# Attention, expert and dense layers in one kernel: one-hot rows by one scaled operation and a transfer, constants in six groups, similarities behind the products with v

## The chip, the cores and the metric

The kernel runs on one core of one Trainium2 chip. Its engines are TensorE (PE, matrix products and transposes), ScalarE (ACT), VectorE (DVE), GpSimd (POOL) and SyncE (SP, which here issues most of the transfers, or DMAs). The metric is the time of one execution on the device in microseconds (us), given as the median of several runs. All engines run their own queues of instructions in order; they wait for each other by semaphores.

## The reference

Three layers follow each other. All numbers are float32.

```python
# attention: 2 batches x 8 heads, 768 tokens, 64 wide, 16 clusters per head
q_assign = argmax(q_n @ c_n.T); k_assign = argmax(k_n @ c_n.T)     # rows normalised
scores = where(q_assign == k_assign, scale * q @ k.T, -1e9)
attn = exp(scores - max(scores)); attn = attn / (attn.sum() + 1e-9)
x = attn @ v                                                      # 1536 tokens x 512
# experts: each token goes to the best of 8
logits = x @ w_gate + modality_bias[modality_id]; e = argmax(logits)
x[t] = softmax(logits)[e] * (relu(x[t] @ w1[e]) @ w2[e])          # 512 -> 1024 -> 512
# dense: four experts, weighted
out = sum over e of p[:, e] * (relu(x @ w1b[e]) @ w2b[e])
```

## The kernel before, in words

Heads are worked on in pairs (p = 0 to 7, heads 2p and 2p+1). For each pair q and k are loaded, transposed on PE (`tr`, tile `pq`), copied by ACT to `xf` and split into a high and a low part in `hl` (ACT makes the high part, L308, DVE the low one). `stack` then copies them by SP's transfers into one stacked operand for each head, `st`: 128 partitions and four slots of 768 columns, so that one matmul over 128 rows and one over 80 give a tile of scores.

The mask sits in the 80-row matmul. `sims` multiplies q and k with the normalised centroids (`pm`), `simn`, `best` and `first` find the best cluster of each token with DVE and POOL, and write its one-hot to `oht`. `troh` transposes that (`po`, 112 rows: 16 for q and 16 for k of each head, at 0, 32, 64 and 96) and writes rows 64 to 79 of `st`: -BIG times q's one-hot in slot 0, and in slot 3 a 1 where the cluster isn't k's. A pair of tokens of unlike clusters so gets -BIG added to its score.

A head has six score tiles of 128 x 768 (`scores`, tile `s`, L406 and L407). For each, DVE takes the maximum (`nm`, L411), ACT the exponential (`e`, L417, with the row sums), PE transposes `e` (`t`, L429), ACT or DVE copy it to `at`, and after six tiles PE multiplies by v (`o`, L446). Score tiles have two buffers in the PSUM memory, so tile i+2 waits until the exponential has read tile i. Names in the traces and lists carry the head and the tile: `s4_0` is head 4, tile 0.

The order is written in a table of steps, `OFF`: six steps are a head, twelve a pair, and `put(step, prio, f)` files each function at a step counted from the start of its pair; within a step the priority decides. From the order in which the functions are then called a list scheduler fixes each engine's queue. `issue_after` adds an order between two instructions, `high_priority` moves instructions ahead. Beside the pairs stands the list `extra`: small constants, the routing of the first batch (transposing x, logits, choice of expert, positions, a scatter through DRAM by POOL), its reading back in sorted order (`reload`, `sorted_xT`). Then come the expert slots (`ph`: w1, `ht`: relu; `pa`, `pb`: w2, L780 to L796) and the dense layer. Its input is prepared during the last expert slot (`dense_x`: `turn` transposes, `sums` are subtractions on POOL at L1008, `ready` casts them on ACT at L1016), by the list `todo`, one entry per stage of that slot.

## Time and profile before

| | |
|---|---|
| median of three runs | 982.63 us (979.29, 982.63, 983.04) |
| profiled execution | 981.43 us, span 979.7 us |
| granted TensorE clock, mean | 0.991 of full speed |
| busy PE, DVE, ACT, POOL | 945.3, 603.4, 476.0, 382.3 us |
| share of the chain that ended last | PE 52%, every other engine 1% or less |
| largest groups on PE | dense layer's second product (L1105) 276.9 us; transposes of `e` 87.7; experts' first product 78.2; score tiles 74.2 and 68.4 |

The span runs from the first to the last instruction. Busy shares are averages over stages of different kind: up to about 300 us the attention, to 486 us mostly the experts, then the dense layer. Idle time of an engine counts only if the engine that sets the end waits for it.

### The profile page before, as it was taken

The page shows a single profiled execution, that of the slowest core. Times are in us where ns is not written, and L with a number is a line of the kernel's source. Part 1 is how long each engine was busy: PE and PEld are TensorE (multiplying, and loading weights), DVE is VectorE, ACT ScalarE, POOL GpSimd, SP SyncE. Part 2 cuts the span into 40 slices and gives each one's busy share as a digit, 9 for nine tenths or more (in the row PEclk, how much of TensorE's full clock was granted, in tenths as well). Part 3 has the DMA queues.
Part 4 walks back from the last instruction along what each step waited for, and adds up shares of the span by engine and source line. Part 5 has one row for each costly group of instructions (what it writes and reads, how often), then busy time and mean ns, then how long its engine had stood idle before and what let it go on. Part 6 is the DMA issues. An engine that isn't in the chain of part 4 may idle for free.

```text
span 979.7 us, 14022 instructions
## 1 busy us (share of the span) xinstructions
PE 945.3 (96%) x5199; PEld 788.5 (80%) x5199; DVE 603.4 (62%) x1050; ACT 476.0 (49%) x920; POOL 382.3 (39%) x404
## 2 busy tenths in 40 slices
PE   8899999989999999989999999999999999999997
PEld 6666766666667788877889989898998989898896
DVE  7876777667775355463666565656766565665654
ACT  7778777767773242354534333343533334343320
POOL 6524531534000400026594544545344544535302
PEclk9999999999999999999999999999999999999999
DMA  8553456076122870266212121222213212212201
GB/s 176 119 133 78 98 130 141 22 198 177 42 88 87 311 235 31 74 215 191 71 62 77 55 85 65 64 66 64 65 65 108 65 65 65 65 65 65 65 1 64
DMA packets 80244, 95.87 MB, mean 98 GB/s; under 512 B 29616, under 2 KB 59824, under 8 KB 80176
## 3 DMA queue, kind: packets, MB, share of 16 engines
q1 hardware_dynamic: 77248, 85.40, 31.0%
q0 software_dynamic: 2784, 9.54, 2.6%
q8 instruction: 41, 0.67, 0.3%
q14 instruction: 27, 0.22, 0.1%
q10 hardware_dynamic: 144, 0.03, 0.0%
HBM read 70.53 MB, written 6.34 MB: 78 GB/s over the span
## 4 chain that ended last, share of the span: by engine, by line
PE 52%; DVE 1%; POOL 1%; DMA 1%; issue 1%; SPq 1%; ACT 0%; POOLq 0%; DVEq 0%; ACTq 0%
PE po L1105 26%; PE px L1057 13%; PE pz L1057 7%; PE py L1057 3%; PE ph L780 1%; DMA rw<-in_moe_w_dram 1%; PE pa L796 1%; POOL out_dram L1142 0%; DVE hd L1064 0%; POOL t L1008 0%; DVE w L749 0%; PE pxT L999 0%; PE pb L796 0%; POOL xf L1008 0%; SPq L921 0%
## 5 line engine op out<-in xcount | busy, mean ns | idle before, releaser
L1105 PE MATMUL po<-w,hd 128*128 128x512 f32 x1152 | 276.9, 393 | 1.3 <-DVE y L1140 1.3
L1105 PEld LDWEIGHTS po<-w,hd 128*128 128x128 f32 x1152 | 215.5, 188 | 46.3 <-DVE y L1140 1.7
L1140 DVE SCALAR_TENSOR_TENSOR y<-po,meta,y 128x512 f32<-128x512 f32 x180 | 132.0, 746 | 56.7 <-PE po L1105 56.7
L1041 POOL TENSOR_TENSOR wa<-rw,wa 128x512 fp32r<-128x512 f32 (+1 forms) x62 | 68.8, 1129 | 173.2 <-PE po L1105 92.0
L411 DVE TENSOR_REDUCE nm<-s 128x1 f32<-128x768 f32 x96 | 91.0, 952 | 27.4 <-PE s L407 26.9
L1040 ACT CAST ws<-sw 128x1024 fp32r<-128x1024 f32 x31 | 32.6, 1050 | 146.4 <-PE po L1105 123.2
L749 DVE TENSOR_TENSOR w<-rw,w 128x1024 fp32r<-128x1024 f32 x63 | 78.4, 1247 | 37.4 <-ACT w L748 37.1
L748 ACT CAST w<-rw 128x1024 fp32r<-128x1024 f32 x63 | 65.8, 1050 | 65.6 <-PE pz L1057 35.1
L417 ACT ACTIVATE e<-s,nm 128x768 f32<-128x768 f32 x96 | 87.3, 909 | 14.8 <-DVE nm L411 13.1
L429 PE MATMUL t<-ident,e 128*128 128x128 f32 x576 | 87.7, 278 | 2.5 <-DVE at L435 1.5
L780 PE MATMUL ph<-x,w 128*128 128x384 f32 x384 | 78.2, 354 | 5.5 <-DVE ht L784 3.0
L406 PE MATMUL s<-st 128*128 128x384 f32 x192 | 74.2, 387 | 9.0 <-ACT e L417 8.4
L429 PEld LDWEIGHTS t<-ident,e 128*128 128x128 f32 x576 | 69.8, 142 | 12.5 <-ACT at L433 3.1
L780 PEld LDWEIGHTS ph<-x,w 128*128 128x128 f32 x384 | 70.5, 197 | 10.1 <-issue 4.5
L1041 POOL TENSOR_TENSOR ws<-sw,ws 128x1024 fp32r<-128x1024 f32 x31 | 74.6, 2407 | 9.9 <-ACT ws L1040 9.4
L1057 PE MATMUL px<-xd,wa 128*128 128x384 f32 x384 | 78.0, 338 | 0.0
L1057 PE MATMUL px<-xd,ws 128*128 128x384 f32 x384 | 77.8, 337 | 0.1
L1057 PE MATMUL pz<-xd,ws 128*128 128x384 f32 x384 | 77.5, 337 | 0.0
L407 PE MATMUL s<-st 80*128 80x384 f32 x192 | 68.4, 357 | 3.6 <-ACT st L396 3.6
L1057 PEld LDWEIGHTS px<-xd,wa 128*128 128x128 f32 x384 | 68.6, 188 | 3.1 <-issue 0.2
L1057 PEld LDWEIGHTS pz<-xd,ws 128*128 128x128 f32 x384 | 68.2, 188 | 2.9 <-ACT xf L1000 0.2
L446 PE MATMUL o<-at,vraw 128*64 128x384 f32 x384 | 70.1, 502 | 0.0
(262 smaller groups left out, 1456.5 us busy)
## 6 DMA issues: line engine op xcount, KB each, us to landing
rw<-in_moe_w_dram SPq DMA_DIRECT2D x94, 512.0 KB, 3.5
st<-hl SPq DMA_DIRECT2D x46, 384.0 KB, 6.9
lw<-in_moe_w_dram SPq DMA_DIRECT2D x16, 512.0 KB, 5.7
xs<-xs_sorted POOLq DMA_DIRECT2D x2, 1560.0 KB
qraw<-in_q_dram SPq DMA_DIRECT2D x16, 192.0 KB, 3.4
kraw<-in_k_dram SPq DMA_DIRECT2D x16, 192.0 KB, 4.0
vraw<-in_v_dram SPq DMA_DIRECT2D x8, 384.0 KB, 4.0
xs_sorted<-x,r_posi POOLq DMA_INDIRECT x12, 7.2
```

What stands on the lines that cost most here:

```text
L406: t.matmul(ps[:, j, 0:384], st[:, 1, qc], st[:, 2, kc], start=True, stop=False)
L407: m = t.matmul(ps[:, j, 0:384], st[0:80, 0, qc], st[0:80, 3, kc], start=False, stop=True)
L411: self.mark = v.tensor_reduce(out=nm, in_=ps[:, :, 0:384], axis=AX.XY, op=ALU.max, negate=True)
L417: a.activation(e, ps[:, :, 0:384], AF.Exp, bias=nm, scale=1.0, accum_out=state[n]["sums"][:, i:i + 1])
L429: self.turned = t.transpose(pt[:, r, :], e[:, j, r * 128:(r + 1) * 128], self.ident)
L446: t.matmul(po[64 * hf:64 * hf + 64], vr[:, r], at[hf][:, r, :], start=(r == 0), stop=(r == R - 1))
L749: self.v.tensor_tensor(out=lo, in0=raw, in1=hi.bitcast(F32), op=ALU.subtract)
L780: t.matmul(ph, w[:, wi, kc, fs], x[:, :, kc, xi, :], start=(m == 0), stop=(m == 11))
L1041: g.tensor_tensor(out=w[:, 1, r], in0=src, in1=w[:, 0, r].bitcast(F32), op=ALU.subtract)
L1057: t.matmul(ps, w[:, wi, 2 * ai + k], xd[bi // 2][:, bi % 2, xi, k], start=start and m == 0, stop=m == 5, skip_group_check=not start)
L1105: t.matmul(p, d["h"][:, 2 * f + j, hi, 128 * i:128 * i + 128], W[2][:, wi, f, :], start=m == 0, stop=m == 5)
L1140: v.scalar_tensor_tensor(out=y, in0=p, scalar=pr, in1=y, op0=ALU.mult, op1=ALU.add)
```

## The change

1. For pairs 1 to 7, `troh` writes the transposed one-hots of all four groups with one ACT operation for each half into a tile `oh` of 112 rows, with a scale per row (`ohs`: -BIG on the rows of q, 1 elsewhere). Four SP transfers of 16 x 768 numbers (48 KB) take them to rows 64 to 79 of the two stacked operands. The copies of `hl` for the second head (`stack(p, 1)`) now come between the two pairs of transfers.
2. The steps: transposes of q and k at -14 and -13 rather than -13 and -12, the first head's stack at -8 rather than -4, the similarities at -12 and behind the last product with v (`self.grouped`), `troh` at -5; reading back, sorted x and the leftovers 3 or 4 steps later, and `sorted_xT` at every second step; the logits in two functions, routing at steps 0, 1, 2, 4, 6, 8 and 10 instead of every second.
3. `best` of pair 6 multiplies on DVE rather than on POOL.
4. The constants that were made at step 2 in one go are made in six groups at steps 3, 6, 9, 17, 20 and 23.
5. `todo` transposes one piece of the dense input per stage rather than two, and starts sums and casts three stages later.

```diff
-OFF = dict(load=-23, loadv=-9, loadv0=-3, norms=-17, tr0=-13, tr1=-12, st0=-4, sims=-11, simn=-9, best=-8,
-           first=-6, st1=-4, troh=-4, sc=-2, ex=-1, tt=0, av=6, fin=11, avn=2, nd=6, tpq=1, tpn=0, tpo=0, tot=0,
+OFF = dict(load=-23, loadv=-9, loadv0=-3, norms=-17, tr0=-14, tr1=-13, st0=-8, sims=-12, simn=-9, best=-8,
+           first=-6, st1=-5, troh=-5, ptroh=7, sc=-2, ex=-1, tt=0, av=6, fin=11, avn=2, nd=6, tpq=1, tpn=0, tpo=0, tot=0,
            pprep=7, pstack=5, pav=5, pfin=7, psc=0, pex=1, ptt=2, pno=8, t00=46, t01=50, t02=53, rs=53, rd=2,
-           rl=66, rld=75, sx=72, lf=83, lo=93, t10=92, s0w=90, s0=95, s0n=4, t13=98)
+           rl=70, rld=78, sx=75, lf=86, lo=93, t10=92, s0w=90, s0=95, s0n=4, t13=98)
...
+        self.ohs = self.const([112, 1], "ohs")
+        g.memset(self.ohs, 1.0)
+        for hh in range(2):
+            g.memset(self.ohs[64 * hh:64 * hh + 16], -BIG)
...
-                    with self.tc.issue_after(self.score[1].ins):
+                    with self.tc.issue_after(self.score[:2][-1].ins):
...
-            for j in range(4):
-                c = slice(384 * (j % 2), 384 * (j % 2) + 384)
-                t.matmul(pm[32 * j:32 * j + 32], cb, d["xf"][:, j // 2, c], start=True, stop=True)
+            with ExitStack() as order:
+
+                if p > 1:
+                    order.enter_context(self.tc.high_priority(offset=200))
+                    order.enter_context(self.tc.issue_after(self.grouped.ins))
+                for j in range(4):
+                    c = slice(384 * (j % 2), 384 * (j % 2) + 384)
+                    t.matmul(pm[32 * j:32 * j + 32], cb, d["xf"][:, j // 2, c], start=True, stop=True)
...
-            (v if p == 0 else g).tensor_tensor(out=sim, in0=sim, in1=self.d16[:, None, :].to_broadcast([128, 4 * R, 16]),
+            (v if p in (0, 6) else g).tensor_tensor(out=sim, in0=sim, in1=self.d16[:, None, :].to_broadcast([128, 4 * R, 16]),
...
         def troh(p):
+            if p:
+                oh = self.tile("s3", [112, S], f"oh{p}", F32R)
             for half in range(2):
                 po = self.ps("MT"[o["tpo"]], [112, HALF, 128], f"po{p}")
                 for j in range(HALF):
                     t.transpose(po[:, j, :], self.oht[:, HALF * half + j, :], self.ident)
                 pf = po.rearrange("p a t -> p (a t)")
                 c = slice(384 * half, 384 * half + 384)
+                if p:
+                    a.activation(oh[:, c], pf, AF.Copy, scale=self.ohs)
+                    continue
                 for hh in range(2):
-                    st = ST[2 * p + hh]
-                    if p == 0 and half:
+                    st = ST[hh]
+                    if half:
                         v.tensor_scalar(out=st[64:80, 0, c], in0=pf[64 * hh:64 * hh + 16], scalar1=-BIG, scalar2=None,
                                         op0=ALU.mult)
                         v.tensor_copy(st[64:80, 3, c], pf[64 * hh + 32:64 * hh + 48])
                     else:
                         a.activation(st[64:80, 0, c], pf[64 * hh:64 * hh + 16], AF.Copy, scale=-BIG)
                         a.copy(st[64:80, 3, c], pf[64 * hh + 32:64 * hh + 48])
+            for hh in range(2 if p else 0):
+                if hh:
+                    stack(p, 1)
+                for slot, r in ((0, 64 * hh), (3, 64 * hh + 32)):
+                    self.after("st", s.dma_start, ST[2 * p + hh][64:80, slot, :].bitcast(F32), oh[r:r + 16, :].bitcast(F32))
...
-                        t.matmul(po[64 * hf:64 * hf + 64], vr[:, r], at[hf][:, r, :], start=(r == 0), stop=(r == R - 1))
+                        self.grouped = t.matmul(po[64 * hf:64 * hf + 64], vr[:, r], at[hf][:, r, :], start=(r == 0), stop=(r == R - 1))
...
-            put(W * p + o["st1"], o["pstack"], lambda p=p: stack(p, 1))
-            put(W * p + o["troh"], o["pprep"], lambda p=p: troh(p))
+            if p == 0:
+                put(W * p + o["st1"], o["pstack"], lambda p=p: stack(p, 1))
+            put(W * p + o["troh"], o["ptroh"] if p else o["pprep"], lambda p=p: troh(p))
...
-            lt_sb = self.tile("s3", [8, 768], f"ltsb{b}")
-            pl = self.ps("M", [128, 384], f"pl{b}")
+            pl = d["pl"] = self.ps("M", [128, 384], f"pl{b}")
             for k2 in range(2):
                 for j in range(4):
                     kc = 2 * (j % 2) + k2
                     t.matmul(pl[32 * j:32 * j + 8], self.wg[:, kc, :], d["xT"][:, kc, 384 * (j // 2):384 * (j // 2) + 384],
                              start=(k2 == 0), stop=(k2 == 1))
+
+        def logits_out():
+            lt_sb, pl = self.tile("s3", [8, 768], f"ltsb{b}"), d["pl"]
...
-        def small():
+        def held(*fs):
             with tc.issue_after(K.mark.ins):
-                K.constants2()
-                K.load_small(wg, mb, mid, dp)
-                K.setup_moe()
-
-        extra = [(2, small)]
+                for f in fs:
+                    f()
+
+        extra = [(3, lambda: held(K.constants2)), (6, lambda: held(K.constants3)), (9, lambda: K.load_small(wg, mb, mid, dp)),
+                 (17, lambda: held(K.setup_moe)), (20, lambda: held(lambda: K.setup_batch(0))),
+                 (23, lambda: held(lambda: K.setup_batch(1)))]
...
-        for i in range(6):
-            extra.append((o["rs"] + o["rd"] * i, lambda i=i: rt[0][1][i]()))
+        for i, n in enumerate((0, 1, 2, 4, 6, 8, 10)):
+            extra.append((o["rs"] + n, lambda i=i: rt[0][1][i]()))
         extra.append((o["rl"], lambda: K.reload(0)))
         extra.append((o["rld"], lambda: K.reloaded(0)))
         for i in range(6):
-            extra.append((o["sx"] + i, lambda i=i: K.sorted_xT(0, i)))
+            extra.append((o["sx"] + 2 * i, lambda i=i: K.sorted_xT(0, i)))
...
-        todo = [turn[:2], st[:1] + turn[2:4], st[1:2] + turn[4:], sums[:1] + ready[:1], sums[1:2], ready[1:2], st[2:3] + sums[2:3],
-                st[3:4] + ready[2:3], sums[3:], ready[3:4], ready[4:5], [], st[4:5] + ready[5:6], st[5:6], st[6:7] + ready[6:]]
+        todo = [turn[:1], st[:1] + turn[1:2], st[1:2] + turn[2:3], turn[3:4], turn[4:5], turn[5:], st[2:3] + sums[:1] + ready[:1],
+                st[3:4] + sums[1:2] + ready[1:2], sums[2:3] + ready[2:3], sums[3:] + ready[3:4], ready[4:5], ready[5:6],
+                st[4:5] + ready[6:], st[5:6], st[6:7]]
```

The first place is SP's queue at pair 4 (heads 8 and 9; `hl4` is the split q and k, `oh4` the new tile). Before:

```order
L75 DMA st8_410_1781<-hl4_336_1488 64x1536
L75 DMA st8_410_1781<-hl4_336_1488 64x2x768
L215 DMA vraw4_374_1639<-in_v_dram 128x2x384
L75 DMA st8_410_1781<-hl4_336_1488 64x1536
L75 DMA st9_411_1785<-hl4_336_1488 64x1536
L75 DMA st9_411_1785<-hl4_336_1488 64x2x768
L75 DMA st9_411_1785<-hl4_336_1488 64x1536
```

After:

```order
L75 DMA st8_384_1662<-hl4_334_1470 64x1536
L223 DMA vraw4_377_1640<-in_v_dram 128x2x384
L75 DMA st8_384_1662<-hl4_334_1470 64x2x768
L75 DMA st8_384_1662<-hl4_334_1470 64x1536
L75 DMA st8_384_1662<-oh4_404_1745 16x768 x2
L75 DMA st9_407_1758<-hl4_334_1470 64x1536
L75 DMA st9_407_1758<-hl4_334_1470 64x2x768
L75 DMA st9_407_1758<-hl4_334_1470 64x1536
L75 DMA st9_407_1758<-oh4_404_1745 16x768 x2
```

Transfers from `oh4` stand behind those of each head, those of the second head behind the first's one-hots.

The second place is ACT at the start of pair 2 (heads 3 and 4; `po2` are the transposed one-hots, `pq3` the transposed q of pair 3). Before:

```order
L417 ACTIVATE e3_4_222_1038,sums3_181_867<-s3_4_211_988,nm3_212_993 128x768
L433 COPY at3_1_223_1040<-t3_3_224_1041 128x3x128
L417 ACTIVATE e3_5_231_1070,sums3_181_867<-s3_5_220_1031,nm3_221_1036 128x768
L449 COPY osb2_226_1057<-o2_200_935 128x384
L395 ACTIVATE st4_216_1007<-po2_219_1023 16x384
L396 CAST st4_216_1007<-po2_219_1023 16x384
L395 ACTIVATE st5_217_1011<-po2_219_1023 16x384
L396 CAST st5_217_1011<-po2_219_1023 16x384
L433 COPY at3_1_223_1040<-t3_4_232_1072 128x3x128
L433 COPY at3_1_223_1040<-t3_5_237_1091 128x3x128
L417 ACTIVATE e4_0_236_1089,sums4_228_1062<-s4_0_229_1063,nm4_230_1068 128x768
```

After:

```order
L440 ACTIVATE e3_5_230_1060,sums3_176_836<-s3_5_219_1021,nm3_220_1026 128x768
L472 COPY osb2_225_1047<-o2_196_918 128x384
L456 COPY at3_1_222_1030<-t3_4_231_1062 128x3x128
L302 COPY xf3_234_1073<-pq3_235_1074 128x384
L302 COPY xf3_234_1073<-pq3_236_1081 128x384
L316 ACTIVATE hl3_233_1072<-xf3_234_1073 128x384 x2
L440 ACTIVATE e4_0_239_1095,sums4_227_1052<-s4_0_228_1053,nm4_229_1058 128x768
L456 COPY at3_1_222_1030<-t3_5_240_1097 128x3x128
L302 COPY xf3_234_1073<-pq3_242_1107 128x384
```

The four operations on 16 rows are gone from here; `xf3` and `hl3` of the next pair have moved ahead of `e4_0`.

The third place is PE at the same point, up to the third score tile of head 4, `s4_2`. Before:

```order
L407 MATMUL s4_0_229_1063<-st4_216_1007 128x384
L406 MATMUL s4_1_234_1082<-st4_216_1007 128x384
L407 MATMUL s4_1_234_1082<-st4_216_1007 128x384
L406 MATMUL s4_1_234_1082<-st4_216_1007 128x384
L407 MATMUL s4_1_234_1082<-st4_216_1007 128x384
L429 MATMUL t3_5_237_1091<-ident_64,e3_5_231_1070 128x128 x3
L429 MATMUL t3_5_238_1096<-ident_64,e3_5_231_1070 128x128 x3
L461 MATMUL ot2_243_1117<-ident_64,osb2_226_1057 128x128 x2
L292 MATMUL pq3_241_1103<-ident_64,qraw3_163_802 128x128 x3
L461 MATMUL ot2_243_1117<-ident_64,osb2_226_1057 128x128
L406 MATMUL s4_2_244_1122<-st4_216_1007 128x384
```

After:

```order
L430 MATMUL s4_0_228_1053<-st4_182_856 128x384
L300 MATMUL pq3_235_1074<-ident_64,qraw3_158_771 128x128 x3
L300 MATMUL pq3_236_1081<-ident_64,qraw3_158_771 128x128 x3
L430 MATMUL s4_1_237_1088<-st4_182_856 128x384
L429 MATMUL s4_1_237_1088<-st4_182_856 128x384
L430 MATMUL s4_1_237_1088<-st4_182_856 128x384
L452 MATMUL t3_5_240_1097<-ident_64,e3_5_230_1060 128x128 x3
L452 MATMUL t3_5_241_1102<-ident_64,e3_5_230_1060 128x128 x3
L484 MATMUL ot2_244_1121<-ident_64,osb2_225_1047 128x128 x3
L429 MATMUL s4_2_248_1138<-st4_182_856 128x384
```

The six transposes of q of pair 3 have moved ahead of the rest of `s4_1`.

The fourth place is ACT in the last expert slot, where the dense input is prepared (`xd` is that input, cast; `t1` and `t2` are POOL's sums; `ht` the relu that PE's second product needs). Before:

```order
L783 ACTIVATE ht_1047_4913<-ph_1046_4900 128x384
L1016 CAST xd0_1063_5011<-t1_1048_4916 128x768
L1016 CAST xd0_1063_5011<-t2_1050_4930 128x768
L1016 CAST xd0_1067_5052<-xf0_1026_4811 128x768
L748 CAST w1_1043_4892<-rw1_1042_4890 128x1024
L1016 CAST xd0_1067_5052<-xf0_1026_4811 128x768
L748 CAST w2_1045_4897<-rw2_1044_4895 128x1024
L783 ACTIVATE ht_1052_4945<-ph_1051_4932 128x384
```

After, the same place of ACT:

```order
L776 CAST w1_1047_4871<-rw1_1046_4869 128x1024
L811 ACTIVATE ht_1055_4929<-ph_1054_4916 128x384
L1028 COPY xf0_1033_4808<-pxT_1056_4932 128x4x128
L776 CAST w2_1049_4876<-rw2_1048_4874 128x1024
L776 CAST w1_1062_4973<-rw1_1061_4971 128x1024
L776 CAST w2_1064_4978<-rw2_1063_4976 128x1024
L958 ACTIVATE hs_1058_4964<-phx_1057_4947 128x256
L1044 CAST xd0_1070_5017<-t1_1059_4966 128x768
L811 ACTIVATE ht_1066_4994<-ph_1065_4981 128x384
L1044 CAST xd0_1070_5017<-t2_1069_5003 128x768
```

The casts of `t1`, `t2` and of two more pieces stood ahead of `ht_1052`; its counterpart, ahead of `hs`, is `ht_1055`, and they now come behind it.

## Rows read from the trace of the kernel before

**Rows 1.** Windows by stage: from:to, length, then busy time by engine, clock, DMA share, GB/s
```profile
0.00:300.00 300.00, 281.28 (x1809) 202.27 (x1810) 216.36 (x455) 219.68 (x474) 109.52 (x158) 0.99 0.50 118
486.00:979.70 493.70, 486.16 (x2412) 435.67 (x2410) 297.22 (x441) 183.90 (x332) 226.89 (x208) 1.00 0.20 64
```
**Rows 2.** Waits of PE up to 490 us: who waits for whom, us in total, times, longest
```profile
PE s L406 <- ACT e L417: 8.4, 13, 2.6
PE s L407 <- ACT st L396: 3.6, 7, 0.6
PE ph L780 <- DVE ht L784: 3.0, 1, 3.0
```
**Rows 3.** Windows behind three idle times, the clock is the third number from the end
```profile
32.00:36.00 4.00, 3.00 (x13) 2.79 (x13) 4.00 (x9) 2.51 (x6) 0.00 (x0) 0.64 0.96 221
218.00:222.00 4.00, 4.00 (x16) 1.67 (x16) 2.00 (x3) 3.03 (x7) 3.92 (x5) 0.64 0.75 200
442.00:446.00 4.00, 3.42 (x11) 3.42 (x12) 2.79 (x4) 1.02 (x2) 2.34 (x2) 0.59 0.98 277
```
**Rows 4.** ACT's groups up to 420 us: count, then busy us, mean ns of one
```profile
L417 ACT ACTIVATE e<-s,nm 128x768 f32<-128x768 f32 x96 | 87.3, 909 | 14.8 <-DVE nm L411 13.1 <-issue 1.1
L395 ACT ACTIVATE st<-po 16x384 fp32r<-16x384 f32 x30 | 14.4, 480 | 1.6 <-PE po L385 1.0
L308 ACT ACTIVATE hl<-xf 128x384 fp32r<-128x384 f32 x28 | 14.1, 544 | 0.0
L294 ACT COPY xf<-pq 128x384 f32<-128x384 f32 x28 | 12.5, 488 | 7.3 <-PE pq L292 7.3
```
**Rows 5.** Timeline, PE at the start of pair 2: start, duration, instruction, idle time before
```profile
80.21 0.82 PE L429 MATMUL t<-ident,e 128*128 128x128 f32 x6
81.60 0.44 PE L407 MATMUL s<-st 80*128 80x384 f32 x1 [0.57 <-ACT st L396]
...
82.58 1.05 PE L429 MATMUL t<-ident,e 128*128 128x128 f32 x6
...
84.54 0.44 PE L406 MATMUL s<-st 128*128 128x384 f32 x1 [0.24 <-ACT e L417]
```
**Rows 6.** Transfers: of st, issue ns and landing us; of xr, KB and landing
```profile
L75 SPq DMA_DIRECT2D st<-hl x36: 461/631/2587, 58.9 to 238.5; - x36
DMA to landing us min/median/max: 4.7/7.0/11.0
...
xr<-xs_sorted SPq DMA_DIRECT2D x2, 64.0 KB, 1.8
```
**Rows 7.** Timeline, the first pair, DVE and PE
```profile
28.48 0.13 DVE L123 TENSOR_SCALAR ti<-pid 48x1 int32<-48x1 int32 x1
31.44 0.92 DVE L411 TENSOR_REDUCE nm<-s 128x1 f32<-128x768 f32 x1
...
30.75 0.44 PE L406 MATMUL s<-st 128*128 128x384 f32 x1 [1.13 <-ACT e L417]
33.06 0.83 PE L429 MATMUL t<-ident,e 128*128 128x128 f32 x3 [1.00 <-DVE at L435]
```
**Rows 8.** Timeline, PE at the logits
```profile
176.23 0.45 PE L406 MATMUL s<-st 128*128 128x384 f32 x1 [1.46 <-ACT e L417]
```
**Rows 9.** Timeline, pair 6
```profile
207.90 2.16 PE L446 MATMUL o<-at,vraw 128*64 128x384 f32 x12
208.71 1.01 POOL L364 TENSOR_TENSOR sim<-sim,d 128x384 f32<-128x384 f32 x1
...
215.92 0.44 PE L406 MATMUL s<-st 128*128 128x384 f32 x1 [2.56 <-ACT e L417]
```
**Rows 10.** Timeline, PE at pair 7
```profile
247.31 0.55 PE L429 MATMUL t<-ident,e 128*128 128x128 f32 x3 [0.95 <-ACT at L433]
```
**Rows 11.** Timeline, the last expert slot
```profile
437.01 0.83 ACT L1016 CAST xd<-xf 128x768 fp32r<-128x768 f32 x1 [1.69 <-POOL xf L1008]
442.58 3.92 PE L780 MATMUL ph<-x,w 128*128 128x384 f32 x12 [3.01 <-DVE ht L784]
```

More of the change, by code (lines that the diff above doesn't have):

```diff
@@ L596, in scatter @@
                                      in_=x[:, r, :], in_offset=None)
-        return turn, [logits, turn_back, choose, gate, place, scatter]
+        return turn, [logits, logits_out, turn_back, choose, gate, place, scatter]
     def setup_moe(self):
         v = self.v
+        v.tensor_copy(self.mid, self.mi.rearrange("p b (r t) -> p b r t", t=2)[:, :, :, 0])
         self.bias = self.const([128, 2, 6, 8], "bias")
-        for b in range(2):
-            t0 = self.tile("s3", [128, 6, 8], "b0")
-            md = self.tile("s3", [128, 2, 6], "md")
-            for i in range(2):
-                v.tensor_scalar(out=md[:, i], in0=self.mid[:, b], scalar1=float(i), scalar2=None, op0=ALU.is_equal)
-            for i, o in ((0, t0), (1, self.bias[:, b])):
-                v.tensor_tensor(out=o, in0=md[:, i, :, None].to_broadcast([128, 6, 8]),
-                                in1=self.mb[:, None, 8 * i:8 * i + 8].to_broadcast([128, 6, 8]), op=ALU.mult)
-            v.tensor_tensor(out=self.bias[:, b], in0=self.bias[:, b], in1=t0, op=ALU.add)
-            sp = self.tile("s3", [128, 6], "sp")
-            v.tensor_reduce(out=sp, in_=self.dp[:, b], axis=AX.X, op=ALU.add)
-            v.tensor_scalar(out=sp, in0=sp, scalar1=1e-9, scalar2=None, op0=ALU.add)
-            v.reciprocal(sp, sp)
-            v.tensor_tensor(out=self.dp[:, b], in0=self.dp[:, b], in1=sp[:, :, None].to_broadcast([128, 6, 4]),
-                            op=ALU.mult)
         self.meta = self.const([128, 12, 8], "meta")
@@ L628, in setup_moe, with setup_batch @@
         self.sel = [None] * 2
+    def setup_batch(self, b):
+        v = self.v
+        t0 = self.tile("s3", [128, 6, 8], "b0")
+        md = self.tile("s3", [128, 2, 6], "md")
+        for i in range(2):
+            v.tensor_scalar(out=md[:, i], in0=self.mid[:, b], scalar1=float(i), scalar2=None, op0=ALU.is_equal)
+        for i, o in ((0, t0), (1, self.bias[:, b])):
+            v.tensor_tensor(out=o, in0=md[:, i, :, None].to_broadcast([128, 6, 8]),
+                            in1=self.mb[:, None, 8 * i:8 * i + 8].to_broadcast([128, 6, 8]), op=ALU.mult)
+        v.tensor_tensor(out=self.bias[:, b], in0=self.bias[:, b], in1=t0, op=ALU.add)
+        sp = self.tile("s3", [128, 6], "sp")
+        v.tensor_reduce(out=sp, in_=self.dp[:, b], axis=AX.X, op=ALU.add)
+        v.tensor_scalar(out=sp, in0=sp, scalar1=1e-9, scalar2=None, op0=ALU.add)
+        v.reciprocal(sp, sp)
+        v.tensor_tensor(out=self.dp[:, b], in0=self.dp[:, b], in1=sp[:, :, None].to_broadcast([128, 6, 4]), op=ALU.mult)
     def reload(self, b):
```

18 lines of the change are left out of this document (10 added, 8 removed).

## The prediction

> **What bounds the kernel now.** I read the windows by stage first. From 486 us to the end TensorE (PE) is busy 486.16 of 493.70 us, and the change touches nothing there; in the first 300 us, the attention, it is busy 281.28 [rows 1]. So the kernel is bound by PE nearly everywhere, and a change that keeps PE's matmuls can win only idle PE time before 486 us, and the slower clock that some of the longer idle times leave behind. The view of waits, read for PE up to 490 us, says whom PE waits for: 8.4 us in 13 times for the exponentials of L417, 3.6 us in 7 times for the one-hot rows written by L396, and once 3.0 us for `ht` of L784 [rows 2]. A timeline of PE's idle times then gives the places: one at the start, one per pair of heads, one at the routing, one at pair 6, one at pair 7, and one where the dense layer's input is prepared. ScalarE (ACT), VectorE (DVE), GpSimd (POOL) and SyncE's queue (SP) count only there.
>
> What a long idle time costs afterwards is seen in three windows: PE's granted clock is 0.64, 0.64 and 0.59 in 32 to 36, 218 to 222 and 442 to 446 us [rows 3]. Four microseconds at 0.64 lose 4 x 0.36 = 1.44 us of PE work, at 0.59 4 x 0.41 = 1.64. Each comes with idle times of 2.1 to 3.0 us (at 32 us two together) [rows 7, 9, 11]; the single one of 1.46 us at 176 us [rows 8] is followed by none.
>
> **One-hots of pairs 1 to 7.** Per pair eight operations of ACT on 16 partitions (4 of L395 and 4 of L396, 0.48 us each [rows 4]; 56 in all) become two on 112 partitions. Their size is that of L294 or L308, 0.488 and 0.544 us [rows 4], so I take 0.5: 56 x 0.48 = 26.9 us of ACT become 14 x 0.5 = 7. ACT is not the bound, so of these 20 us only what PE waited for counts. In a pair that is 0.57 us at the second matmul of the pair's first scores, and 0.24 us at its third score tile, 0.81 together [rows 5].
>
> What is new on that path: `oh`, then SP's transfers to the stacked operand. In the new order PE has, between the last `po` transposes of pair 2 and the first L407 of head 4 (which reads the one-hots), six transposes (0.82), the scores of head 3's last tile (five such matmuls took 81.60 to 82.58, so about 0.8 for four), six transposes again (0.82), half an AV product (half of 2.16), a single matmul (0.2), six transposes (0.82) and another single one (0.2): 4.7 us by [rows 5, 9], and about 0.4 more for the short waits on exponentials between them that remain. ACT has one exponential (0.9) ahead of the second `oh` and ends it at about 1.1 after those transposes. SP's two transfers are issued behind it; an issue like it takes 0.46 to 0.63 [rows 6], so the second starts at about 1.6. A landing of up to 5.1 - 1.6 = 3.5 us is hidden. No row shows a 48 KB copy within the on-chip memory. From below there are the 64 KB of `xr`, 1.8 us; from above the 384 KB of `st<-hl`, 4.7 at best, 7.0 in the median, 11.0 at most [rows 6]. I take 2, near the row of like size: hidden, with 1.5 us to spare, cost 0. Without the cover it is (7.0 - 3.5) x 7 = 24.5 us.
>
> The order of the queue speaks against this: in pair 7 two weight loads of 512 KB stand just ahead of the transfers, larger than the transfers that needed 4.7 to 11.0 [rows 6]. If these come first, the one-hots of pair 7 land at 4.7 to 7.0 instead of 2, and PE waits 1.2 to 3.5 us there, once; this is a rival below. The Trainium skill, "DMA: Bandwidth & Descriptors", section "Queues, rings and completion order", says that each transfer engine takes a queue's descriptors in ring order, which is this mechanism; its section on the anatomy of one DMA gives about 2.0 us fixed and bytes over 436 GB/s, an estimate of 2.1 us for 48 KB, with which the sum would be the same. The row of `xr` agrees with the second; no row shows the first alone.
>
> Behind SP's wait for `oh` stand the three large transfers of the pair's second head (moved behind it), its own one-hots and the next pair's loads. The second head starts six tiles later; 96 tiles [rows 4] fill some 280 us [rows 1], 2.9 each, so 17 us later, which with the 5.1 above leaves 22 us, against some 1.6 + 5 issues x 0.6 + 11.0 = 15.6. Hidden. The loads are for the pair after.
>
> **The new wait in the pair.** The q transposes of the next pair now stand right behind the first scores, and ACT does both `xf` and both `hl` of them before the exponential that frees the buffer for the third score tile. From the end of the first scores PE has six `pq` transposes (0.82), three matmuls (0.6), six `t` (0.82) and `ot` (0.4 to 0.5): about 2.7 us. ACT's chain is the transposes (0.82), the second `xf` (0.49), two `hl` (1.09) and the exponential (0.91): 3.3 us [rows 4, 5]. That leaves a wait of 0.6. If DVE's `nm` or the first `xf` come later, it is up to 1.0; if they overlap better, 0.4. Against the 0.81 removed the seven pairs give from 7 x 0.4 = 2.9 gained to 7 x 0.2 = 1.4 lost. I take 0.8, so 0: the walk leaves out semaphore delays, and those are always on the late side.
>
> **Constants in six groups, transposes in another order at the start.** Before, some thirty small DVE operations run from 28.48 on, and the maximum `nm` starts only at 31.44; PE idles 1.13 and 1.00 us, and the slow stretch of 1.44 follows [rows 3, 7]. The groups put them at steps 3, 6, 17, 20 and 23, a few tenths to 1 us of DVE each. Most of 3.57 us should go; the first pair's own waits come in part instead. I take 2.0 (0 to 3.6).
>
> **Logits in two steps.** At 176.23 PE waits 1.46 us, for an exponential that ACT has behind the copy of the logits [rows 8]. This exponential is now ahead of that copy; two later ones stand behind the copy and the `oh` of pair 5, and PE loses about half of the time there. Taken 0.7 (0 to 1.5).
>
> **Pair 6's multiplication on DVE.** POOL is issuing the scatter and starts L364 at 208.71 only; PE's products there run 207.90 to 210.06, and the transposes of the one-hots and with them ACT's four L395 and L396 fall late, ahead of an exponential: PE waits 2.56 us at 215.92 [rows 9], and 1.44 us go in the slow stretch behind it [rows 3]. On DVE it takes about 0.55, and does not wait for POOL; the block of four on ACT is gone as well. Of 4.0 us I take 3.4, leaving one new wait of 0.6 as above (2.0 to 4.0).
>
> **sorted_xT every second step.** The idle time of 0.95 at 247.31 [rows 10] and smaller ones beside it: taken 1.0 (0 to 1.5).
>
> **Dense input one turn per step.** ACT stood 1.69 us waiting for POOL's `xf` to cast it at 437.01, with `ht` queued behind, so PE waited 3.01 at 442.58 [rows 11], plus 1.64 of slow clock [rows 3]. In the new order that `ht` has no cast of POOL's results ahead. Two later ones have; the second needs the result of POOL that now stands behind a sum of the dense weights. Of 4.65 I take 3.8 (1 to 4.6).
>
> **The sum.** 0 + 0 + 2.0 + 0.7 + 3.4 + 1.0 + 3.8 = 10.9 us. The profiled execution took 981.43 (span 979.7), so 970.5; against the median of the runs, 982.63, which is 1.2 higher, it would be 971.7. I say 971. About 0.5%, 4.9 us, is what a measurement of this kernel can tell from no change: faster is below 977.7, slower above 987.5.
>
> **Rivals.**
> - *One-hots late in every pair (slower).* Place: the first L407 of each pair. If the 48 KB transfers queue behind the 384 KB ones like those behind each other, 7.0 us, PE waits 3.5 us seven times, 24.5, and with idle times that long the clock falls each time, up to 7 x 1.44 = 10: 971 + 24.5 to 34.5 = 995 to 1005. It eats the whole gain from 10.9 / 7 = 1.6 us a pair, a landing of 5.1, and makes it slower by the bound from about 5.9. For: no such row, and the median of 7.0. Against: in most pairs the large ones ahead were issued some 10 us before. Chance 0.14 (0.02 of it within 0.5%).
> - *ACT's block of `xf` and `hl` is not hidden at all (no change).* The whole block of 2 x 0.49 + 2 x 0.54 = 2.06 us shows instead of 0.6 to 0.8, in seven pairs: 7 x 1.25 = 8.8, so 980. For: the exponentials are what PE waits for most [rows 2]. Against: PE has 2.7 us of other work there. Chance 0.19 (0.16 within, 0.03 faster with half of it).
> - *Queue order in pair 7 alone.* 1.2 to 3.5 us and a slow stretch of 1.44: 973 to 976. Chance 0.10, faster.
> - *The dense wait moves to a later `ht`.* The 3.8 are not won: 975. Chance 0.12, faster.
> - *The forecast*, 965 to 975 by itself: chance 0.45.
>
> Faster is 0.45 + 0.12 + 0.10 + 0.03 = 0.70, the same 0.16 + 0.02 = 0.18, slower 0.12. The lower end is 962, if the pairs give 2.9 and the start, the logits, pair 6, pair 7 and the dense input their upper ends, together 7.2 us more, and 1.8 for small idle times that I have not priced; the upper end is 984, which takes in the second rival and leaves out most of the first.
>
> **What would show it.** In the changed profile: 14 rows of the new activation of about 0.5 us; the transfers from `oh` landing near 2 us, and no idle time of PE at the first L407 (now L430) of a pair, but one of 0.6 to 0.8 at the third tile's L406 (now L429), for the exponential; no block of small DVE operations at 28 to 32 us and a clock near 1 behind; no idle time of 2.56 in pair 6; `ph` near 440 us without its 3.0 and at full clock. From 486 us on, the same 493 us. It is wrong if transfers from `oh` land over 3.5 us after their issue, or if idle times of over 1.5 us appear at new places, since the clock falls behind them too.

## The result and the profile after

The changed kernel took 971.18 us in the median of four runs, before 982.84: a ratio of 0.9882 (0.9853 to 0.9911). Beside the experiments it ran twice more, with ratios of 0.9925 (0.9899 to 0.9952) and 0.9898 (0.9875 to 0.9920); its single runs spread from 968.8 to 976.7. The forecast was 971, a gain of 10.9; the three differences of medians are 11.7, 7.5 and 10.1. Medians are of all runs, while ratios and their intervals leave out runs that are over 1.5% above the fastest of their kernel. The profiled execution took 973.57 with a span of 971.9, so it shows 7.8 us of the gain; another profile of the same kernel (e12) has a span of 968.7.

DVE takes one maximum `nm` per score tile, 96 in all in both kernels. Their starts, counted from tile 0, give marks that run through the attention. With them, and with three marks that both kernels have (the end of the 2.14 us idle time at the head of the last expert slot, the first wait of `py`, the end), the gain splits so (us; "gain" is before less after, "gain, e12" before less e12):

| stretch | before | after | e12 | gain | gain, e12 | forecast |
|---|---|---|---|---|---|---|
| start to tile 9 (head 1) | 40.94 | 37.17 | 37.95 | 3.8 | 3.0 | 2.0 |
| to tile 54 (head 9), four pairs | 124.21 | 123.07 | 123.11 | 1.1 | 1.1 | 0 |
| to tile 69, logits | 45.87 | 44.53 | 44.54 | 1.3 | 1.3 | 0.7 |
| to tile 75, pair 6 | 22.10 | 17.33 | 17.34 | 4.8 | 4.8 | 3.4 |
| to tile 93, pair 7 and reading back | 47.86 | 52.25 | 51.87 | -4.4 | -4.0 | 1.0 |
| to the last expert slot | 136.78 | 140.91 | 137.30 | -4.1 | -0.5 | 0 |
| last slot, dense input | 59.67 | 55.85 | 55.83 | 3.8 | 3.8 | 3.8 |
| dense layer | 502.3 | 500.8 | 500.8 | 1.5 | 1.5 | 0 |
| all | 979.7 | 971.9 | 968.7 | 7.8 | 11.0 | 10.9 |

So the total was right while several of its terms were not; that of the reading back had the wrong sign. The waits of PE up to 490 us, who waits for whom, us in total, times, longest, answer to [rows 2]:

```profile
PE s L429 <- ACT e L440: 9.9, 19, 0.8
PE pa L824 <- ACT ht L811: 5.0, 1, 5.0
PE pxT L680 <- DMA xs<-xs_sorted: 4.1, 1, 4.1
PE pa L824 <- DVE ht L812: 2.2, 1, 2.2
```

The wait for the one-hots (L396 before, 3.6 us) and that of 3.0 for `ht` at `ph` are gone; the one for the exponentials grew from 8.4 to 9.9 but holds none over 0.8. New are one of 4.1 for the rows read back and one of 2.2 for `ht` at `pa`; the one of 5.0 was 2.0 before (e1). In the timeline of PE (start, duration, instruction, idle time before) of the changed kernel, the first two rows answer to [rows 7], the next two to [rows 5], the last to [rows 8]:

```profile
31.32 0.44 PE L429 MATMUL s<-st 128*128 128x384 f32 x1 [0.36 <-ACT e L440]
33.52 0.55 PE L452 MATMUL t<-ident,e 128*128 128x128 f32 x3 [0.57 <-ACT at L456]
...
77.58 0.34 PE L430 MATMUL s<-st 80*128 80x384 f32 x1
...
81.27 0.45 PE L429 MATMUL s<-st 128*128 128x384 f32 x1 [0.82 <-ACT e L440]
...
171.70 0.44 PE L429 MATMUL s<-st 128*128 128x384 f32 x1 [0.66 <-ACT e L440]
```

The first L430 of a pair, which needs the one-hots, no longer waits; the third tile waits 0.82 instead of 0.24: 0.57 + 0.24 was exchanged for 0.82. That is pair 2; the third tile of pair 4 waits 0.34, that of pair 7 not at all, the others 0.81 to 0.82. The new operation, in the view of the tile `oh` (count, then shortest, median and longest in ns):

```profile
L404 ACT ACTIVATE oh<-po,ohs x14: 578/580/582, 38.1 to 245.9; 112x384 fp32r<-112x384 f32 x14
```

Its transfers, in the page's list of transfers (count, size, median us to landing):

```profile
st<-oh SPq DMA_DIRECT2D x28, 48.0 KB, 3.6
```

The operation takes 0.58 us (0.5 was taken). The 3.6 is the median of all 28. The fourteen for a pair's first head, those that the next scores need, land after 2.1 to 3.4, most after 2.1; the fourteen for the second head, issued right behind three copies of 384 KB, after 3.9 to 5.9.

Reading the sorted rows back is where part of the gain was lost. In the kernel before, POOL issues the load `xs` just ahead of the norms of pair 7 (L244), and PE comes to the rows without a wait:

```profile
218.06 0.94 POOL L633 DMA_DIRECT2D xs<-xs_sorted  x1 [8.34 <-PE t L429]
219.91 1.47 POOL L244 TENSOR_TENSOR sq<-qraw 128x768 f32<-128x768 f32 x1
230.39 0.60 PE L652 MATMUL pxT<-ident,xs 128*128 128x128 f32 x4
```

In the changed kernel:

```profile
205.80 0.78 POOL L664 DMA_DIRECT2D es<-xs_sorted  x1 [4.32 <-DMA xs_sorted<-x,r_posi]
214.62 4.20 POOL L237 TENSOR_TENSOR rq<-rq,half 128x24 f32<-128x24 f32 x1
219.41 0.95 POOL L661 DMA_DIRECT2D xs<-xs_sorted  x1 [0.25 <-issue]
...
232.79 0.79 PE L680 MATMUL pxT<-ident,xs 128*128 128x128 f32 x4 [4.09 <-DMA xs<-xs_sorted]
```

The scatter had landed by 205.8, but the load stands behind the norms of pair 7 on POOL and is issued 13.6 us later, no earlier than before; PE, which is 11 us earlier than before at tile 75, stands still for it. The windows behind it and behind the next long wait, clock third from the end, answer to [rows 3] (0.50 is the lower of the clock's two levels, 1.2 GHz, all through; 0.64 is part at that level):

```profile
232.00:236.00 4.00, 3.21 (x15) 3.15 (x16) 1.75 (x3) 1.70 (x3) 0.00 (x0) 0.64 0.00 1
336.00:340.00 4.00, 3.23 (x9) 2.94 (x10) 1.98 (x3) 0.99 (x3) 0.00 (x0) 0.50 0.94 337
```

### The profile page after: what moved, and what is told of

Its sections match the earlier page's. It is cut to its first block, busy times and chain, and to the rows that moved or that the text cites. A ratio compares the mean times of both kernels' runs of the same rounds, so it can differ in the third digit from the quotient of the medians.

```text
span 971.9 us, 14024 instructions
## 1 busy us (share of the span) xinstructions
PE 935.1 (96%) x5199; PEld 785.1 (81%) x5199; DVE 611.1 (63%) x1051; ACT 457.1 (47%) x878; POOL 386.0 (40%) x406
## 4 chain that ended last, share of the span: by engine, by line
PE 53%; DVE 2%; POOL 1%; issue 1%; ACT 0%; POOLq 0%; ACTq 0%; DVEq 0%
PE po L1133 26%; PE px L1085 13%; PE pz L1085 7%; PE py L1085 3%; PE ph L808 1%; PE pa L824 1%; DVE xd L1045 1%; PE pxT L1027 1%; DVE hd L1092 1%; POOL out_dram L1170 1%; DVE w L777 0%; PE pb L824 0%; POOL xf L1036 0%; POOL t L1036 0%; ACT w L776 0%
## 5 line engine op out<-in xcount | busy, mean ns | idle before, releaser
L777 DVE TENSOR_TENSOR w<-rw,w 128x1024 fp32r<-128x1024 f32 x63 | 80.9, 1286 | 45.3 <-ACT w L776 45.0
L452 PE MATMUL t<-ident,e 128*128 128x128 f32 x576 | 83.8, 276 | 1.5 <-ACT at L456 0.8
L808 PE MATMUL ph<-x,w 128*128 128x384 f32 x384 | 76.1, 348 | 2.1 <-issue 2.1
L808 PEld LDWEIGHTS ph<-x,w 128*128 128x128 f32 x384 | 68.5, 193 | 6.5 <-issue 4.5
L430 PE MATMUL s<-st 80*128 80x384 f32 x192 | 68.2, 355 | 0.4 <-ACT st L414 0.4
```

The lines of the kernel that those rows point to most:

```text
L430: m = t.matmul(ps[:, j, 0:384], st[0:80, 0, qc], st[0:80, 3, kc], start=False, stop=True)
L452: self.turned = t.transpose(pt[:, r, :], e[:, j, r * 128:(r + 1) * 128], self.ident)
L777: self.v.tensor_tensor(out=lo, in0=raw, in1=hi.bitcast(F32), op=ALU.subtract)
L808: t.matmul(ph, w[:, wi, kc, fs], x[:, :, kc, xi, :], start=(m == 0), stop=(m == 11))
```

## The experiments

**e1, e12: the changed kernel again.** No edit.

> The changed kernel once more, as the reference for the others. In its first profile TensorE waits 5.02 us at 336.77 for ht, because a weight load issued 0.4 us before a load of 1560 KB landed after 10.6 us; before the change that wait was 2.03. Theory: which of the two transfers comes first is decided by less than a microsecond, so the wait lies between 2 and 5 here, and the time between 968.5 and 973.5. Rival: the change fixes the order; the wait is 5.0 again.

> The changed kernel again, beside e10 and e11 on the same chip. 969 to 974, with a wait for ht in the third expert slot anywhere between 1.4 and 5.4 us, as in the ten profiles so far.

Measured: 973.20 and 973.28 us, spans of 968.3 and 968.7. The wait for `ht` in the third expert slot was 5.02 in the first profile, 2.47 and 2.34 in these:

```profile
334.56 0.73 PE L824 MATMUL pa<-w,ht 128*128 128x512 f32 x2 [2.34 <-ACT ht L811]
```

Over all fourteen profiles of this study, of kernels with or without the change, it lies between 1.40 and 5.40. ACT's `ht` stands behind the cast of a weight whose 512 KB load is issued 0.7 to 1.8 us ahead of the 1560 KB load of the second batch, in every one of the fourteen. So their order does not decide, though the expectation had it so: in the first profile and in e12 the lead is 1.2 us, and the load landed after 11.2 and after 6.0. What makes it land late is not shown. The wait is not the change's; it makes up most of the difference between the two profiles (row "to the last expert slot").

**e2: the load issued earlier.**
```diff
-           rl=70, rld=78, sx=75, lf=86, ...
+           rl=66, rld=78, sx=75, lf=86, ...
```

> As the changed kernel, but the sorted rows are read back at step 66 as before the change, not 70: POOL issues that load right behind the scatter, ahead of the norms of pair 7. Theory: the wait of 4.09 us at 232.79 is the lateness of that load (issued at 219.41 behind 13 us of norms); it goes, with the slow clock behind it (1.44 + 0.28): 5.8 less, about 965.5. Rival: the load is slow whatever its issue (13.2 us landing beside the stacks), the wait stays over 2 us or moves to another place: 969 to 972.

Measured: 974.13, ratio 0.9924 (0.9895 to 0.9952), no gain. The wait at `pxT` is gone, and as long a one has come at the one-hots of pair 6:

```profile
206.58 0.90 POOL L661 DMA_DIRECT2D xs<-xs_sorted  x1 [4.62 <-PE po L400]
208.14 1.21 SPq L75 DMA_DIRECT2D st<-oh  x2
...
217.24 0.69 PE L430 MATMUL s<-st 80*128 80x384 f32 x1 [4.09 <-DMA st<-oh]
```

The small transfers, issued 1.6 us behind 1560 KB, land after 8.4 to 9.8 us; at the same place of the changed kernel it was 2.1 for the first head's. This is what the prediction's slower rival feared, late one-hots, at one place and through another queue: not the order in SP's queue, but a large load from POOL's.

**e8: the rows used later.**
```diff
-           rl=70, rld=78, sx=75, lf=86, ...
+           rl=70, rld=78, sx=77, lf=88, ...
```

> The changed kernel, with the transposes of the sorted rows two steps later (77) and the leftovers too (88); the load itself as it is. Theory: PE no longer reaches them before the load has landed at 232.7: the wait of 4.09 and its slow stretch go, 5.8 us: 965 to 967. Rival: they now collide at the end of the attention with the work of the second batch, and the gain is lost there: 970 to 973.

Measured: 963.94, ratio 0.9853 (0.9818 to 0.9887). Of the 4.09 us 1.09 are left, and the clock stays up:

```profile
232.97 0.66 PE L680 MATMUL pxT<-ident,xs 128*128 128x128 f32 x4 [1.09 <-DMA xs<-xs_sorted]
```

Tile 93 comes at 269.24, 5.1 us ahead of the changed kernel (first row the changed kernel, second e8):

```profile
274.35 0.95 DVE L434 TENSOR_REDUCE nm<-s 128x1 f32<-128x768 f32 x1
269.24 0.95 DVE L434 TENSOR_REDUCE nm<-s 128x1 f32<-128x768 f32 x1
```

The stretch from tile 75 takes 46.69 us, 1.2 less than before the change. e11 has the same edit and the same effect (tile 93 at 269.98). The traces show the gain more clearly than the runs do: the interval of e8 still overlaps that of the first measurement (0.9853 to 0.9911), and its profile met the shortest of all waits in the third slot, 1.40. With e2: at step 66 the load hits the one-hots (the steps between 66 and 70 were not run), but its use can be later.

**e3: the one-hots by eight operations again, all else as changed.**
```diff
-                if p:
-                    a.activation(oh[:, c], pf, AF.Copy, scale=self.ohs)
-                    continue
...
                         a.activation(st[64:80, 0, c], pf[64 * hh:64 * hh + 16], AF.Copy, scale=-BIG)
                         a.copy(st[64:80, 3, c], pf[64 * hh + 32:64 * hh + 48])
...
```

The four transfers go too, and the second head's copies are again filed by themselves.

> As the changed kernel, but the one-hots of pairs 1 to 7 are written by eight ScalarE operations each as before, without the transfers; all else as changed. Theory (ScalarE's chain ahead of the third tile's exponential sets the wait of 0.8 there): 1.9 us of operations come back ahead of xf, hl and the exponential, of which ScalarE's idle 0.6 takes a part; the wait grows to 1.5 to 2.3, 7 x 1.1 = 8 us more, about 979. Rival (the prediction's own term: the one-hots cost and give nothing by themselves): 969 to 973.

Measured: 989.85, slower than before (1.0066, 1.0036 to 1.0096) and more than either theory said. At tile 66 it is 10.3 us behind the changed kernel, near the theory's 8; the rest comes behind it, where PE waits 8.4 for the rows read back instead of 4.1. The waits in the pairs are not where the theory put them: up to 300 us PE waits 4.3 for `at` and 4.2 for the old one-hots to leave their PSUM buffers, while those for the exponentials fall to 7.3. With the transposes and stacks moved ahead, ACT seems to have no room for the eight operations.

**e6: the one-hots alone, on the kernel before.** The edit is that of the change's `troh`, with every step as before.

> The kernel before, with the one-hots by scaled operations and transfers alone; all steps as before. Theory: the 0.57 at the pair's first L407 goes and the 0.24 at the third tile stays or goes, 4 to 5.7 us in seven pairs: 976 to 978. Rival A (it needs the first head's stack to be copied earlier, at -8, which this kernel lacks: the one-hots queue behind 384 KB transfers and land after 4.7 to 7): waits of 1 to 3.5 us at the first L407, 988 to 1005. Rival B (as the prediction's sum had it, gain and new waits cancel): 980 to 983.

Measured: 985.67, 1.0054 (1.0021 to 1.0086), longer than rival B's 983. In the profile (span 980.1) tile 54 comes at 165.49, before at 165.15, so rival B held in the pairs: the waits of 0.57 and 0.24 became one at the third tile,

```profile
53.07 0.44 PE L420 MATMUL s<-st 128*128 128x384 f32 x1 [1.51 <-ACT e L431]
```

six times, of 1.5 to 1.9 us, and PE did not wait for the transfers. The order is not quite that of before, either: the similarities `pm` (e7) stand in three pieces fewer, which gives 2.5 us back. Three runs took 990 to 994 us at a mean granted clock of 0.979 to 0.982, where the profiled one has 0.993; slow stretches behind these waits would fit that, but no such run was profiled. e3 and e6 together: the one-hots by themselves gain nothing, and the other steps without them lose.

**e4: the first head's one-hots issued last.**
```diff
-            for hh in range(2 if p else 0):
+            for hh in (1, 0) if p else ():
```

> As the changed kernel, but the transfers of the first head's one-hots are issued last, behind the three of 384 KB and the one-hots of the second head. Theory (the landing is hidden with some 2.5 us to spare): issued five issues (3.3 us) later and landing after 4 to 5.6 rather than 2.1, they come 5 to 7 us later, so the first L430 of a pair waits 2.5 to 4.5 us, seven times: 18 to 31 us more, and up to 10 for the slow clock: 989 to 1012. Rival (more cover than that, or small transfers overtake the large ones): 971 to 975.

Measured: 985.39, 1.0020 (0.9988 to 1.0051), by the ratios some 9 us slower than the changed kernel, but not as said. The copies of 384 KB do not wait for `oh`, so they went ahead: at pair 3 the last of them was issued at 101.13 and had landed when the four transfers from `oh` were issued from 111.66 on. These landed after 2.1 to 3.0 us. PE waits at the third tile (1.5 to 2.7 us, six times), not at L430, in another order of PE (the profiled run took 995.15). So the edit did not make the test that it was meant for, and how much cover the landing has is not measured here.

**e7: the transposes of q and k at their old steps.**
```diff
-tr0=-14, tr1=-13,
+tr0=-13, tr1=-12,
```

> The changed kernel, with the transposes of q and k at the steps of before (-13 and -12). In its order the exponential of a pair's first tile is ahead of xf and hl again. Theory: the wait of 0.82 at the third tile falls to 0.24 or less, 7 x 0.6 = 4 us: some 969 where the changed kernel has 971 to 973. Rival: the wait moves to a later tile of the same head (similarities and one-hots come later), 971 to 974.

Measured: 973.48, 0.9935 (0.9914 to 0.9956); the span of its profile is 977.0. The wait at the third tile did fall to 0.24, yet tile 54 comes at 165.89, 5.7 us later than in the changed kernel. Neither theory names why: 3.8 us of the 5.7 arise in the four pairs from tile 9 on, the rest ahead of them. In the pairs the similarities `pm` explain it: busy time of their 64 matmuls up to 300 us in before, after and e7 (a fence each; count, then busy us):

```profile
L331 PE MATMUL pm<-xf,cb 128*32 128x384 f32 x64 | 12.2, 498 | 0.2 <-ACT xf L294 0.2
```
```profile
L344 PE MATMUL pm<-xf,cb 128*32 128x384 f32 x64 | 9.3, 498 | 0.0
```
```profile
L344 PE MATMUL pm<-xf,cb 128*32 128x384 f32 x64 | 19.6, 498 | 0.3 <-ACT xf L302 0.2
```

A pair's four products go to four groups of 32 columns. In one piece they take 0.85 us, in two 1.67, in three 2.50, whatever the piece holds. The changed kernel has them in one piece in pairs 2 to 7, before in two in four of these pairs, e7 in three. Eight pieces more between tiles 9 and 54 are 6.6 us, of which the shorter waits give some back. Later e7 gains: it comes to the rows read back at 236.95, when they have landed, and has no wait there.

**e9: the rule for the similarities alone, on the kernel before.**
```diff
...
+                if p > 1:
+                    order.enter_context(self.tc.high_priority(offset=200))
+                    order.enter_context(self.tc.issue_after(self.grouped.ins))
...
```

> The kernel before, with only the new rule for the similarities: their matmuls wait for the last product with v and have high priority. In its order the four matmuls of a pair then stand in three pieces (2, 1, 1) in pairs 2 to 6, where before has two (1, 3; one piece in pair 5). Theory: what the similarities cost is 0.83 us for each piece, because four matmuls on four groups of columns run side by side only if nothing stands between them (0.85 us in one piece, 1.67 in two); six pieces more make 5 us more, 985 to 987 where before has 981. Rival: a piece costs only its matmuls, the rule moves nothing that matters, 980 to 982; or being early gains, 976 to 979.

Measured: 986.32, 1.0034 (1.0012 to 1.0055), span 985.3 against 979.7, and tile 93 4.9 us later (285.84 against 280.98). `pm` is up by the 5 us that six more pieces should cost:

```profile
L336 PE MATMUL pm<-xf,cb 128*32 128x384 f32 x64 | 17.1, 498 | 0.2 <-ACT xf L294 0.2
```

So the price goes by the number of pieces. The rule saves time only where q and k are both transposed by then, which the steps -14 and -13 see to.

**e10: the constants in one go.** The changed kernel with all groups at step 2; the small loads no longer wait for the copies to `st`.

> The changed kernel, with the constants made in one go at step 2 as before (the small loads with them). Theory: the block of DVE operations at 28 us is back, with 1.1 and 1.0 us of idle time and the slow stretch in place of 0.36 and 0.57: 2.5 to 3 us lost at the second head; the wait of 1.08 at 77 us and 0.65 at 73, which the later groups cause, go: 1 to 1.7 back. In all 1 to 2 slower than the changed kernel run beside it. Rival: the groups gain nothing at the start (the first pair's own order sets it): 1 to 2 faster.

Measured: 976.34, beside it the changed kernel 973.28. In the profile:

```profile
31.21 0.69 PE L429 MATMUL s<-st 128*128 128x384 f32 x1 [2.41 <-ACT e L440]
36.21 0.55 PE L452 MATMUL t<-ident,e 128*128 128x128 f32 x3 [0.85 <-DVE at L458]
```

At tile 9 it is 3.6 us behind e12 (41.59 against 37.95), at tile 30 2.1 (97.64, 95.51): the groups gain 3.6 at the start and give 1.5 back in pair 2. First theory, a little larger: 2.5 are left at tile 93 (277.35, 274.81). The two medians differ by 3.1, with intervals that overlap (0.9908 to 0.9958, 0.9875 to 0.9920).

**e5: the dense input alone, on the kernel before.** The edit is the change's `todo`.

> The kernel before, with the new list for the dense input alone (one turn per stage, sums and casts three stages later). Theory: the stretch from the idle time of 2.14 (issue) to the one before py, 59.7 us before and 55.8 after the whole change, falls by the same 3.8 here: the wait of 3.01 and its slow stretch go, one of 2.2 at a later ht comes. About 978 where before has 981 to 982. Rival: the 3.8 come from elsewhere (other transfers, earlier weights); the stretch stays over 58.5.

Measured: 980.20, 0.9992 (0.9971 to 1.0013). The stretch of the last slot is 55.79 us in the profile, as in the changed kernel, 3.9 less than before; the profile lost that to 5.40 of the wait in the third slot. But the interval leaves a gain of at most 2.8, so 3.9 is not what the list gives on average. The profiles say why. With the new list the slot took 55.8 us in five of them (after, e1, e3, e5, e12), 57.2 to 57.4 in three (e2, e8, e10) and 58.8 in two (e4, e7), with none, one and two stretches at the lower clock in it; with the old list (before, e6, e9) 59.2 to 59.7, each with two or one of twice the length. The clock, third number from the end, right behind the same idle time of 2.14 us, in before, after and e8:

```profile
418.00:422.00 4.00, 4.00 (x18) 3.90 (x18) 0.41 (x2) 0.49 (x1) 0.00 (x0) 0.60 0.96 315
416.00:420.00 4.00, 4.00 (x26) 3.83 (x24) 0.88 (x2) 1.97 (x3) 0.00 (x0) 1.00 0.98 316
405.00:409.00 4.00, 4.00 (x18) 3.93 (x17) 0.14 (x1) 0.67 (x2) 0.00 (x0) 0.61 0.98 325
```

The means, 56.9 for the new list and 59.4 for the old, differ by 2.5 us.

**e11: e8, with the last wait of the dense input taken out.** In the list `todo` the last casts move by one stage (not two, as the expectation has it), and DVE's part of them stands behind the `ht` ahead of it. In the changed kernel a wait of 2.16 us follows in that slot, because `ht` on DVE is queued behind two subtractions:

```profile
444.17 3.99 DVE L1045 TENSOR_TENSOR xd<-xf,xd 128x768 fp32r<-128x768 f32 x2
444.81 2.53 POOL L1036 TENSOR_TENSOR t<-xf,t 128x768 f32<-128x768 f32 x1
...
448.08 0.54 DVE L812 SCALAR_TENSOR_TENSOR ht<-ph,ht 128x384 fp32r<-128x384 f32 x1
448.68 0.50 PE L824 MATMUL pa<-w,ht 128*128 128x512 f32 x1 [2.16 <-DVE ht L812]
```
```diff
...
+                if b == 0 and n >= 4:
+                    order.enter_context(self.tc.issue_after(self.mark.ins))
+                v.tensor_tensor(out=lo, in0=src(), in1=hi.bitcast(F32), op=ALU.subtract)
...
```

> The kernel of e8 (sorted rows two steps later), with the last casts of the dense input two stages later and their DVE part behind the ht ahead of it. Theory: the wait of 2.16 at pa in the last expert slot is ht on DVE behind two subtractions that take 4 us beside POOL's; it goes: 961 to 963. Rival: ACT's ht behind the cast of t4 ends no earlier, the wait stays: 964 to 966.

Measured: 967.25, 0.9834 (0.9809 to 0.9860), beside it the changed kernel with 0.9898 (0.9875 to 0.9920). The wait is gone:

```profile
441.30 0.56 DVE L812 SCALAR_TENSOR_TENSOR ht<-ph,ht 128x384 fp32r<-128x384 f32 x1 [0.55 <-ACT ht L811]
...
445.06 1.15 PE L808 MATMUL ph<-x,w 128*128 128x384 f32 x5 [0.18 <-DVE ht L812]
```

The last slot takes 54.1 us (465.94 less 411.82). This version beats both kernels. It is not faster than e8 by this measurement (their intervals overlap); its profile met 5.10 us of the third slot's wait, that of e8 1.40. Which of its two new edits took the wait out was not separated.

## Why the prediction was right, and where it was not

- **Bound.** The prediction let the change win PE's idle time before 486 us and the slow clock behind it, and nothing else ("keeps PE's matmuls"). Most of the gain came the other way: in the first profile PE's busy time fell by 10.2 us (945.3 to 935.1), while its idle time rose from 34.5 to 36.8; in e12 they are 935.3 and 33.4. The idle times that went were replaced by the 4.1 for the rows, the 2.2 at `pa` and, in the first profile, 3 us more in the third slot. Of the busy time some 3 to 4 us are the slow clock that was priced (the mean granted clock is 0.991 before, 0.994 and 0.995 after). The rest is the same products in less time: 2.9 us less for `pm`, 1.5 in the dense layer, and most of 3.9 for the transposes of `e` (83.8 us against 87.7, part of it the clock). These stand in larger groups: 117 pieces where there were 131; six in one piece take 0.82, three 0.49.
- **One-hots of pairs 1 to 7, new wait in the pair.** Priced at 0 together: removed 0.81, added 0.8; the trace has 0.81 and 0.82 at pair 2. The landing was taken as 2 us and is 2.1 to 3.4 for the first heads, with no wait at L430 in pairs 1 to 7. (The estimate of 2.1 us beside it was for transfers that GpSimd issues, and these are SP's; the trace decides.) The zero of the four pairs became 1.1: three pieces of `pm` fewer give 2.5, and the late constants take 1.5 back (e7, e9, e10).
- **Queue order in pair 7.** No wait: the first head's transfers, issued from 246.52 on, land after 2.1 us though two weight loads of 512 KB were issued from 242.76 on. The mechanism that the prediction feared is real, but not there: behind the 384 KB copies the second heads' transfers take 3.9 to 5.9 us, which stays hidden, and beside the 1560 KB load 8.4 to 9.8, which does not (e2). The Trainium skill, "DMA: Bandwidth & Descriptors", section "Queues, rings and completion order", also says that a transfer engine goes round the queues packet by packet. e2 fits that as far as a load in POOL's queue slowed those in SP's; the turns themselves no run here shows.
- **Start.** 2.0 taken, 3.0 to 3.8 measured, above the end of 3.6 in one profile: I kept too much of the two idle times; 0.36 and 0.57 were left, and no slow stretch (clock 1.00 from 32 to 36 us).
- **Logits, pair 6.** The logits were taken as 0.7 and gave 1.3; pair 6 was taken as 3.4 and gave 4.8, of which about 0.7 is a group of `pxT` that moved behind tile 75.
- **Sorted_xT every second step: the step that failed.** Forecast 1.0 gained, measured 4.0 to 4.4 lost. It looked at PE's idle times near 247 us and priced only the use of the rows. The change also moved the load (66 to 70), and on POOL that is from right behind the scatter to behind the norms of pair 7. I neither looked up POOL's order there nor asked when PE, 11 us earlier, would want the rows. e8 and e11 show that this was the cause, since with the rows used later the stretch takes 1.2 us less than before, near the term's 1.0; e2 shows that moving the load back to step 66 alone does not help.
- **Dense input.** 3.8, and 3.8 measured, but the agreement is luck. The later wait that I foresaw is there and larger (2.16, where 0.85 was allowed), with another cause: not POOL's sum, but DVE's slow subtractions. What made up for it is a second slow stretch of the slot, at 418 us before, that the sum had not counted and that happened to be absent in the three profiles of the changed kernel. Over all profiles the list is worth some 2.5 us (e5).
- **Dense layer.** 1.5 us less in the same matmuls, where the prediction had none. It is there in every run built on the changed kernel (500.4 to 501.4 us) and in none of the kernel before with one part of the change (e5, e6, e9: 502.3 to 502.5). The cause stays open.
- **What would show it wrong.** Two of these signs did appear. The median landing of the transfers from `oh` is 3.6 us, over 3.5, but those over it are the second heads', which are hidden. And idle times of over 1.5 us appeared at new places, 4.09 and 2.16. The clock did not fall behind each of them: behind 4.09 it was 0.64, but behind 2.16 in the last slot of the first profile it was 1.00.
- **Why the total fits.** Five us less than forecast at the reading back are about what the start, the pairs, the logits, pair 6 and the dense layer gave beyond their terms (5.6 us in e12). That part is luck.

## What to carry to other kernels

When an engine gets earlier, go through everything it will want earlier, loads on other queues above all, and find their place in the order of the queue that issues them. Look at PE's busy time as well as its idle time: the order of the same matmuls changes it. Count the pieces in which matmuls on column groups stand, not only the matmuls. Where a time depends on a slow stretch that comes in one execution and not in the next, take it from several profiles. A small transfer is as quick as the large ones beside it let it be: keep bulk loads of any queue away from the microseconds in which a short one is on the path.
